# Attention and MLP on one core: the softmax divisor moved to the AV output, scores in three passes

## The chip, the cores and the metric

The kernel runs on one core of one Trainium2 chip. The metric is device time of one execution in microseconds; the median of 3 runs before the change is 752.19 (751.31 to 752.32).

## The reference

Attention over 4 batches, 8 heads, 576 positions and 64 features, with a learned bias of the relative position, and then a two-matrix MLP. Inputs and output are float32.

```
scores = q @ k^T / 8 + bias[h]        # bias[h,i,j] = relu(x*w1+b1) @ w2, x = log1p|i-j| / log1p(max(i,1))
attn   = exp(scores - rowmax)
attn   = attn / (sum(attn) + 1e-9)
x      = attn @ v                     # heads side by side: 2304 rows of 512
out    = (s * relu(x @ w_in)^2 + b) @ w_out     # 512 -> 2048 -> 512
```

## The kernel before

Everything stands in one program whose order on each engine is the order written (a manual schedule); no engine reorders, and all the DMAs named here are issued by SyncE, one after the other.

*Preparation.* The bias is made in 36 stages of 16 rows. A stage (`bias_features`, `bias_step`) makes four feature tiles on VectorE, GpSimd or ScalarE, multiplies them on TensorE (L135, L138), brings the result through ScalarE into a staging tile `stg` (L142) and stores it to `bias_d` in DRAM (L143). Features are written two stages ahead. A table `plan` puts loads and the first two units of attention behind given stages. `load_bias` brings one head's bias back from DRAM: four blocks of 128 rows into `bt`, and the last 64 rows, doubled over the two halves of the partitions, into `be`.

*Attention.* Work goes by pair: one head and two batches, 16 pairs. The two batches lie in the two halves of the partitions of q and k. A pair has five units: units 0 to 3 are 128 query rows of both batches (two score tiles from the 64-row halves of the array), unit 4 the remaining 64 rows of both batches in one tile. `step(n)` does in this order: scores of unit n+2 on TensorE (`scores`, L196); their scaling, bias and row minimum on VectorE (`biased`, L212); the divisor of unit n+1 (`norm`: add, reciprocal, on VectorE, L231 and L232) and its multiplication into the exponents on GpSimd (`norm_scale`, L237); the transposes of unit n on TensorE with their evictions (`probs_t`, L250 to L271: one small transpose evicted by ScalarE, then four evicted by ScalarE, then four evicted by VectorE); the exponents of unit n+2 on ScalarE with their sums (`expo`, L221); a part of the AV product of the pair before (`av`, L283, L286); one or two pieces of weight decoding (`fill`); and loads for later pairs. The transposes share two PSUM buffers, the score tiles two, the AV product has one. At the end of a pair's AV product ScalarE copies it out (L290) and it is stored to DRAM as `xt_d`.

*MLP.* `expand` (L379) and `project` (L403) use three matmuls for each product, of parts that are rounded to a shorter float (F32R) and their remainders. Its weights are decoded and split during attention.

Of the kernel before, what the change touches and what calls it, by code (L numbers as in the profile page):

```python
# [9 lines left out]
F32 = mybir.dt.float32  # L10
# [16 lines left out]
def attention_moe(ctx, tc, q, k, v, w_in, w_out, dist, par, out):  # L27
# [98 lines left out]
    def bias_step(st):  # L126
        f2, f0, f3, f1 = feats.pop(st)
        fs = (f0, f1, f2, f3)
        if st % 3 == 2:
            ps = ps_x.tile([128, 2, 512], F32, tag="x", name="bps")  # L130
        else:
            ps = ps_s.tile([128, 2, 512], F32, tag="s", name="bps")
        pb = ps.rearrange("p a b -> p (a b)")
        for c in range(4):
            nc.tensor.matmul(  # L135
                pb[32 * c:32 * c + 32, 0:512], w2bd, fs[c][0][:, 0:8], start=True, stop=True)
        for c in range(4):
            nc.tensor.matmul(  # L138
                pb[32 * c:32 * c + 32, 512:S], w2bd, fs[c][0][:, 8:9], start=True, stop=True)
        kcol = kc[:, 1:2] if fs[3][1] else kc[:, 0:1]  # L140
        stg = fp.tile([128, S], F32, tag="stg", name="stg", bufs=10)
        nc.scalar.activation(stg, pb[:, 0:S], AF.Identity, scale=nr[:, st:st + 1], bias=kcol)  # L142
        nc.sync.dma_start(out=bias_d[:, 16 * st:16 * st + 16, :].rearrange("h r j -> r h j"), in_=stg)  # L143

# [2 lines left out]


    qs, ks, vals, tts, bts, pts, units, accs = {}, {}, {}, {}, {}, {}, {}, {}

    def load_bias(p, t0, t1):
        h = pairs[p][0]
        if t0 == 0:
            bts[p] = (io.tile([128, 4, S + 64], F32, tag="bt", name="bt"),
                      io.tile([128, S], F32, tag="be", name="be"))
        bt, be = bts[p]
        if t1 <= 4:
            rows = bias_d[h, 128 * t0:128 * t1, :].rearrange("(t p) j -> p t j", p=128)  # L160
            nc.sync.dma_start(out=bt[:, t0:t1, 64:], in_=rows)
            nc.sync.dma_start(out=bt[:, t0:t1, 0:64], in_=rows[:, :, 512:S])
        else:
            nc.sync.dma_start(
                out=be, in_=bias_d[h, 512:S, :].unsqueeze(0).broadcast_to([2, S - 512, S]))

    def load_q(p):
        if p < NP:
            h, b0 = pairs[p]
            qs[p] = io.tile([128, 640], F32, tag="qt", name="qt", bufs=3)  # L170
            nc.sync.dma_start(out=qs[p], in_=q[b0 // 2, h])

    def load_k(p):
        if p < NP:
            h, b0 = pairs[p]
            ks[p] = io.tile([128, S + 64], F32, tag="kt", name="kt", bufs=3)
            nc.sync.dma_start(out=ks[p], in_=k[b0 // 2, h])

    def load_v(p):
        if p < NP:  # L180
# [5 lines left out]
    def scores(n):  # L186
        p, t = divmod(n, 5)
        qt, kt = qs[p], ks[p]
        c = slice(128 * t, 128 * t + 128)
        xs = range(width(n))  # L190
        ps = [ps_s.tile([128, 2, 512], F32, tag="s", name="sps") for _ in xs]
        for hf in range(2):
            for x in xs:
                d = slice(64 * x, 64 * x + 64) if t < 4 else slice(0, 128)
                o = hf * HALF + (64 if x == 0 else 0)
                nc.tensor.matmul(  # L196
                    ps[x][:, hf, 0:HALF], qt[d, c], kt[d, o:o + HALF], start=True, stop=True)
        units[n] = (
            tp.tile([128, 2, S], F32, tag="pr", name="pr"),
            sm.tile([128, 2], F32, tag="mn", name="mn"),  # L200
            sm.tile([128, 2], F32, tag="su", name="su"),
            sm.tile([128, 2], F32, tag="rs", name="rs"),
            ps,
        )

    def biased(n, x):
        p, t = divmod(n, 5)
        _, mn, _, _, ps = units[n]
        bt, be = bts[group[p]]
        bias = bt[:, t, 64 - 64 * x:64 - 64 * x + S] if t < 4 else be  # L210
        tt = tp.tile([128, S], F32, tag="tt", name="tt")
        nc.vector.tensor_tensor_reduce(  # L212
            tt.rearrange("p (a b) -> p a b", a=2), ps[x][:, :, 0:HALF],
            bias.rearrange("p (a b) -> p a b", a=2),
            -1.0 / ROOT, BIG, ALU.add, ALU.min, mn[:, x:x + 1],
        )
        tts[n, x] = tt

    def expo(n, x):
        pr, mn, su, _, _ = units[n]  # L220
        nc.scalar.activation(  # L221
            pr[:, x], tts.pop((n, x)), AF.Exp, bias=mn[:, x:x + 1], scale=-1.0,
            accum_out=su[:, x:x + 1])

    def width(n):
        return 2 if n % 5 < 4 else 1

    def norm(n):
        _, _, su, rs, _ = units[n]
        c = slice(0, width(n))  # L230
        nc.vector.tensor_scalar(su[:, c], su[:, c], 1e-9, None, op0=ALU.add)  # L231
        nc.vector.reciprocal(rs[:, c], su[:, c])  # L232

    def norm_scale(n, x):
        pr, _, _, rs, _ = units[n]
        r = rs[:, x:x + 1]
        nc.gpsimd.tensor_scalar(pr[:, x], pr[:, x], r, 1.0, op0=ALU.mult, op1=ALU.mult)  # L237

    def probs_t(n, part):
        p, t = divmod(n, 5)  # L240
# [7 lines left out]
        if t < 4 and part < 2:  # L248
            for kb in range(4):
                nc.tensor.transpose(  # L250
                    ps[:, 128 * kb:128 * kb + 128],
                    pr[:, part, 64 * part + 128 * kb:64 * part + 128 * kb + 128], ident)
            o, i = pt[:, :, part, c], ps.rearrange("p (a b) -> p a b", a=4)
            if part == 0:
                nc.scalar.activation(o, i, AF.Copy)
            else:
                nc.vector.tensor_copy(o, i)  # L257
        elif t < 4:
            nc.tensor.transpose(ps[:, 0:128], pr.rearrange("p x j -> p (x j)")[:, 512:640], ident)  # L259
# [12 lines left out]

    def av(p, kb, hf):
# [12 lines left out]
            nc.tensor.matmul(ps[:, hf, 0:HALF], vt[:, 8:10].rearrange("p i d -> p (i d)"), ptr[:, c],  # L286
                             start=False, stop=True)
        if kb == 4 and hf == 1:
            xs = tp.tile([128, S], F32, tag="xs", name="xs", bufs=1)
            nc.scalar.activation(xs.rearrange("p (a b) -> p a b", a=2), ps[:, :, 0:HALF], AF.Copy)  # L290
            nc.sync.dma_start(out=xt_d[b0 // 2][:, h * D:(h + 1) * D, :], in_=xs)


# [127 lines left out]
    for p, (h, _) in enumerate(pairs):  # L421
        group.append(next(i for i, e in enumerate(pairs) if e[0] == h))
        if group[p] == p and p > 0:
            loads_at[p - 2, 2] = ((p, 0, 4), (p, 4, 5))

    def step(n):
        p, u = divmod(n, 5)
# [19 lines left out]
        if p >= 1:  # L447
# [2 lines left out]
            fill()  # L450
            if u % 2 == 0:
                fill()
        if n < LAST:
# [21 lines left out]
    def fill():  # L475
# [23 lines left out]
    }  # L499
    for st in range(STEPS):  # L500
        if st + 2 < STEPS:
# [47 lines left out]
    op = ctx.enter_context(tc.tile_pool(name="op", bufs=2, reuse_waits="tile"))  # L549
    wa = ctx.enter_context(tc.tile_pool(name="wa", bufs=1, reuse_waits="tile"))  # L550
    for kind in range(2):
        alloc_w(w_hi, kind, 1, wa)
# [11 lines left out]
        next(work)  # L564
    pctx.close()
    ps_ctx.close()
    w2 = ctx.enter_context(tc.tile_pool(name="w2", bufs=1, reuse_waits="tile"))
    for kind in range(2):
        alloc_w(w_hi, kind, 2, w2)
# [97 lines left out]
```

## Time and profile before

| | |
|---|---|
| median of 3 runs | 752.19 us |
| profiled execution | 752.64 us |
| its span | 750.8 us |
| mean granted clock of TensorE | 0.993 of full |
| preparation | 0 to about 54 us |
| attention | to about 348 us |
| MLP | to the end |
| TensorE, weight loads, VectorE, ScalarE, GpSimd busy | 97%, 70%, 58%, 50%, 29% of the span |

The page gives shares of the whole span. TensorE's ends are modelled, so that a start of the next group of instructions is the better measure of a duration than a busy time. "Idle before" is followed by what released the engine. Lines L*n* are lines of the kernel before.

### The profile page before, as it was taken

Reading aid. Unit: us, or ns where it says so; the run is one execution under the profiler, and the core shown is the slowest. Engines: PE = TensorE matmul, PEld = TensorE weight load, DVE = VectorE, ACT = ScalarE, POOL = GpSimd, SP = SyncE. Lnnn points to the kernel's source line nnn. Section 1 sums busy time; section 2 is a strip of 40 time slices with the busy share of each in tenths; the row PEclk is TensorE's granted clock in tenths of the full one; section 3 lists DMA queues with packets and bytes.
Section 4 is the critical chain, followed back from the end, with each engine's and each line's share of the span. In section 5 each row is a group of like instructions: output and inputs, shape, how many; then the busy total and the mean of one; then the engine's idle time right before and its main releaser. Section 6 shows DMA issues by size and latency. Waiting matters only on the chain.

```text
span 750.8 us, 11513 instructions
## 1 busy us (share of the span) xinstructions
PE 730.1 (97%) x4226; PEld 526.9 (70%) x4226; DVE 431.9 (58%) x890; ACT 375.1 (50%) x772; POOL 218.7 (29%) x274
## 2 busy tenths in 40 slices
PE   8985999999999999999999999999999999999998
PEld 4443665666666666656888888888888888888896
DVE  7973778888878787883379732233322333223332
ACT  7983677677777777775444422223222232222332
POOL 7962455465445444452664200000000000000000
PEclk9997999999999999999999999999999999999999
DMA  5996344446354654224012130000300002000100
GB/s 170 289 334 198 129 148 160 168 140 196 112 203 130 213 179 180 69 66 142 13 57 81 33 101 12 1 1 0 113 1 0 1 0 85 1 0 1 57 1 28
DMA packets 36056, 71.56 MB, mean 95 GB/s; under 512 B 7712, under 2 KB 10912, under 8 KB 36000
## 3 DMA queue, kind: packets, MB, share of 16 engines
q1 hardware_dynamic: 35856, 70.51, 28.3%
q8 instruction: 33, 0.54, 0.3%
q10 hardware_dynamic: 144, 0.33, 0.1%
q14 instruction: 23, 0.19, 0.1%
HBM read 50.77 MB, written 20.05 MB: 94 GB/s over the span
## 4 chain that ended last, share of the span: by engine, by line
PE 82%; DVE 7%; DMA 3%; ACT 3%; POOL 2%; issue 1%; POOLq 0%; ACTq 0%; DVEq 0%
PE hps L379 27%; PE o L403 27%; PE sps L196 9%; PE xps L283 8%; PE tps L250 6%; PE bps L135 3%; DVE tt L212 3%; POOL pr L237 2%; DMA bias<-stg 2%; PE tps L259 1%; DMA be<-bias 1%; ACT pr L221 1%; ACT stg L142 1%; DVE full L329 1%; PE xps L286 1%
## 5 line engine op out<-in xcount | busy, mean ns | idle before, releaser
L403 PE MATMUL o<-who,gt 128*128 128x512 f32 x576 | 192.4, 393 | 0.0
L379 PE MATMUL hps<-x,whi 128*128 128x512 f32 (+1 forms) x640 | 183.7, 371 | 0.0
L384 DVE SCALAR_TENSOR_TENSOR r<-r,sb 128x512 f32<-128x512 f32 (+1 forms) x80 | 56.8, 709 | 193.5 <-ACT r L383 193.5
L383 ACT ACTIVATE r<-hps 128x512 f32<-128x512 f32 (+1 forms) x80 | 44.4, 555 | 221.9 <-PE hps L379 221.9
L237 POOL TENSOR_SCALAR pr<-pr,rs 128x576 f32<-128x576 f32 x144 | 109.4, 771 | 145.6 <-DVE rs L232 113.5
L379 PEld LDWEIGHTS hps<-x,whi 128*128 128x128 f32 x640 | 116.9, 188 | 23.9 <-issue 0.4
L403 PEld LDWEIGHTS o<-who,gt 128*128 128x128 f32 x576 | 108.2, 188 | 24.1
L221 ACT ACTIVATE pr<-tt,mn 128x576 f32<-128x576 f32 x144 | 110.7, 771 | 20.2 <-DVE su L231 15.8
L379 PE MATMUL hps<-x,wli 128*128 128x512 f32 (+1 forms) x320 | 118.7, 371 | 0.0
L196 PE MATMUL sps<-kt,qt 64*128 64x288 f32 (+1 forms) x576 | 108.4, 433 | 9.7 <-DVE mn L212 9.4
L403 PE MATMUL o<-wlo,gt 128*128 128x512 f32 x288 | 113.2, 393 | 0.0
L212 DVE CUSTOM_DVE_ANT_0 tt<-sps,bt 128x576 f32<-128x576 f32 x128 | 95.6, 747 | 25.9 <-PE sps L196 25.8
L196 PEld LDWEIGHTS sps<-kt,qt 64*128 64x128 f32 (+1 forms) x576 | 62.6, 188 | 51.2 <-DVE mn L212 17.5
L389 DVE SCALAR_TENSOR_TENSOR gt<-r,sb,gt 128x512 fp32r<-128x512 f32 (+1 forms) x80 | 56.3, 703 | 54.2 <-ACT gt L388 54.2
L388 ACT ACTIVATE gt<-r,sb 128x512 fp32r<-128x512 f32 (+1 forms) x80 | 54.4, 681 | 52.5 <-DVE r L384 52.5
L250 PE MATMUL tps<-ident,pr 128*128 128x128 f32 x512 | 77.2, 282 | 1.5 <-ACT ptr L260 1.5
L283 PE MATMUL xps<-pt,vt 128*64 128x288 f32 x512 | 75.8, 418 | 0.0
L379 PEld LDWEIGHTS hps<-x,wli 128*128 128x128 f32 x320 | 60.1, 188 | 10.9
L250 PEld LDWEIGHTS tps<-ident,pr 128*128 128x128 f32 x512 | 57.7, 142 | 13.4 <-ACT ptr L260 12.5
L403 PEld LDWEIGHTS o<-wlo,gt 128*128 128x128 f32 x288 | 54.1, 188 | 11.7
L283 PEld LDWEIGHTS xps<-pt,vt 128*64 128x64 f32 x512 | 31.2, 136 | 23.9 <-issue 10.8
L257 DVE COPY pt<-tps 128x512 f32<-128x512 f32 x64 | 44.0, 687 | 5.8 <-PE tps L250 5.0
(63 smaller groups left out, 700.1 us busy)
## 6 DMA issues: line engine op xcount, KB each, us to landing
bias<-stg SPq DMA_DIRECT2D x36, 288.0 KB
raw<-in_moe_w_in_dram SPq DMA_DIRECT2D x16, 512.0 KB
raw<-in_moe_w_out_dram SPq DMA_DIRECT2D x16, 512.0 KB
bt<-bias SPq DMA_DIRECT2D x7, 1152.0 KB
qt<-in_q_dram SPq DMA_DIRECT2D x16, 320.0 KB
kt<-in_k_dram SPq DMA_DIRECT2D x16, 320.0 KB
vt<-in_v_dram SPq DMA_DIRECT2D x16, 320.0 KB
xt<-xs SPq DMA_DIRECT2D x16, 288.0 KB
```

The costliest lines, as they stand in the source:

```text
L196: nc.tensor.matmul(ps[x][:, hf, 0:HALF], qt[d, c], kt[d, o:o + HALF], start=True, stop=True)
L212: nc.vector.tensor_tensor_reduce(tt.rearrange("p (a b) -> p a b", a=2), ps[x][:, :, 0:HALF], bias.rearrange("p (a b) -> p a b", a=2), -1.0 ...
L221: nc.scalar.activation(pr[:, x], tts.pop((n, x)), AF.Exp, bias=mn[:, x:x + 1], scale=-1.0, accum_out=su[:, x:x + 1])
L237: nc.gpsimd.tensor_scalar(pr[:, x], pr[:, x], r, 1.0, op0=ALU.mult, op1=ALU.mult)
L250: nc.tensor.transpose(ps[:, 128 * kb:128 * kb + 128], pr[:, part, 64 * part + 128 * kb:64 * part + 128 * kb + 128], ident)
L283: nc.tensor.matmul(ps[64 * x:64 * x + 64, hf, 0:HALF], vt[:, 4 * x + kb, :], pt[:, kb, x, c], start=(kb == 0), stop=False)
L379: nc.tensor.matmul(ps[:, 0:n], w[0, g][:, a, fc], xs_t[c, a][:, j, 0:n], start=(i == 0), stop=(i == 3 * KB - 1))
L383: nc.scalar.activation(r, ps[:, 0:n], AF.Relu)
L384: nc.vector.scalar_tensor_tensor(r, r, sb[:, 0:1], r, op0=ALU.mult, op1=ALU.mult)
L388: nc.scalar.activation(hi, r, AF.Identity, bias=sb[:, 1:2])
L389: nc.vector.scalar_tensor_tensor(lo, r, sb[:, 1:2], hi.bitcast(F32), op0=ALU.add, op1=ALU.subtract)
L403: nc.tensor.matmul(os_t[c][i], gt[:, a, tok], w[1, g][:, fo], start=(f == 0 and j == 0), stop=(f == NF - 1 and j == 2))
```

## The change

The scores are made from q and k split into a rounded part and a remainder: three passes in place of one float32 matmul; the splits are made on GpSimd, two for each pair. The probabilities stay undivided through transposes and AV product. The nine columns of sums of a pair are inverted once (`norm`, in the step of unit 3), transposed on TensorE (`norm_t`), copied out by VectorE, stored to DRAM (`norm_store`), loaded back spread over 64 partitions for each batch (`norm_load`, in the step of unit 4) and multiplied into the AV product as it leaves PSUM, on VectorE, in place of ScalarE's copy. The bias tile's last 64 rows are loaded once per head, as two transfers of 64 rows; for the first head, stages 24 to 35 are sent directly from the staging tile (`first_head`). Loads of the preparation are moved, q and k have two buffers in place of three, and the output pool is opened later.

```diff
@@ bias_step
+        if st >= 24:
+            first_head(st, stg)
         nc.sync.dma_start(out=bias_d[:, 16 * st:16 * st + 16, :].rearrange("h r j -> r h j"), in_=stg)
+    def first_head(st, stg):
+        bt, be = bts[0], bes[0]
+        t, r0 = divmod(16 * st, 128)
+        rows = stg[0:128:H, :]
+        if t < 4:
+            nc.sync.dma_start(out=bt[r0:r0 + 16, t, 64:], in_=rows)
+            nc.sync.dma_start(out=bt[r0:r0 + 16, t, 0:64], in_=rows[:, 512:S])
+        else:
+            for x in range(2):
+                nc.sync.dma_start(out=be[64 * x + r0:64 * x + r0 + 16, :], in_=rows)
@@ loads
-            nc.sync.dma_start(
-                out=be, in_=bias_d[h, 512:S, :].unsqueeze(0).broadcast_to([2, S - 512, S]))
+    def load_be(p):
+        if p == 0:
+            bes[0] = io.tile([128, S], F32, tag="be", name="be", bufs=1)
+        elif p < NP and pairs[p][0] == pairs[p - 1][0]:
+            bes[p] = bes[p - 1]
+        elif p < NP:
+            bes[p] = io.tile([128, S], F32, tag="be", name="be", bufs=1)
+            for x in range(2):
+                nc.sync.dma_start(out=bes[p][64 * x:64 * x + 64, :], in_=bias_d[pairs[p][0], 512:S, :])
-            qs[p] = io.tile([128, 640], F32, tag="qt", name="qt", bufs=3)
+            qs[p] = io.tile([128, 640], F32, tag="qt", name="qt")
-            ks[p] = io.tile([128, S + 64], F32, tag="kt", name="kt", bufs=3)
+            ks[p] = io.tile([128, S + 64], F32, tag="kt", name="kt")
+    def split_qk(p, which):
+        if p < NP:
+            full = (qs, ks)[which][p]
+            t = io.tile([128, 2, 640], F32R, tag=f"r{which}", name="qr" if which == 0 else "kr")
+            nc.gpsimd.tensor_scalar(t[:, 0], full, 1.0, 1.0, op0=ALU.mult, op1=ALU.mult)
+            nc.gpsimd.tensor_tensor(t[:, 1], full, t[:, 0].bitcast(F32), op=ALU.subtract)
+            (qs, ks)[which][p] = t
@@ scores
+        mms = []
         for hf in range(2):
             for x in xs:
                 d = slice(64 * x, 64 * x + 64) if t < 4 else slice(0, 128)
                 o = hf * HALF + (64 if x == 0 else 0)
-                nc.tensor.matmul(
-                    ps[x][:, hf, 0:HALF], qt[d, c], kt[d, o:o + HALF], start=True, stop=True)
+                for i, (a, b) in enumerate(((0, 0), (0, 1), (1, 0))):
+                    mms.append((i, hf, x, ps[x][:, hf, 0:HALF], qt[d, a, c], kt[d, b, o:o + HALF]))
+        for i, _, _, o, a, b in sorted(mms, key=lambda e: e[1::-1]):
+            nc.tensor.matmul(o, a, b, start=(i == 0), stop=(i == 2))
@@ divisor
-    def norm(n):
-        _, _, su, rs, _ = units[n]
-        c = slice(0, width(n))
-        nc.vector.tensor_scalar(su[:, c], su[:, c], 1e-9, None, op0=ALU.add)
-        nc.vector.reciprocal(rs[:, c], su[:, c])
-    def norm_scale(n, x):
-        pr, _, _, rs, _ = units[n]
-        r = rs[:, x:x + 1]
-        nc.gpsimd.tensor_scalar(pr[:, x], pr[:, x], r, 1.0, op0=ALU.mult, op1=ALU.mult)
+    def norm(p):
+        su = sums.pop(p)
+        nc.vector.tensor_scalar(su, su, 1e-9, None, op0=ALU.add)
+        nc.vector.reciprocal(su, su)
+        rows[p] = su
+    def norm_t(p, ps):
+        nc.tensor.transpose(ps[0:9, 128:256], rows.pop(p), ident)
+        rt = sm.tile([9, 128], F32, tag="rt", name="rt", bufs=2)
+        nc.vector.tensor_copy(rt, ps[0:9, 128:256])
+        rts[p] = rt
+    def norm_store(p):
+        rt = rts.pop(p)
+        for x in range(2):
+            nc.sync.dma_start(
+                out=rs_d[p][x, 0:512].rearrange("(t j) -> t j", j=128), in_=rt[4 * x:4 * x + 4, :])
+            nc.sync.dma_start(out=rs_d[p][x:x + 1, 512:S], in_=rt[8:9, 64 * x:64 * x + 64])
+    def norm_load(p):
+        rbs[p] = tp.tile([128, S], F32, tag="rb", name="rb", bufs=2)
+        for x in range(2):
+            nc.sync.dma_start(out=rbs[p][64 * x:64 * x + 64, :], in_=rs_d[p][x:x + 1, :].broadcast_to([D, S]))
@@ probs_t
             nc.scalar.activation(ptr[:, c], ps[:, 0:128], AF.Copy)
+            if t == 3:
+                norm_t(p, ps)
@@ av
-            xs = tp.tile([128, S], F32, tag="xs", name="xs", bufs=1)
-            nc.scalar.activation(xs.rearrange("p (a b) -> p a b", a=2), ps[:, :, 0:HALF], AF.Copy)
+            xs = rbs.pop(p)
+            xv = xs.rearrange("p (a b) -> p a b", a=2)
+            nc.vector.tensor_tensor(xv, ps[:, :, 0:HALF], xv, op=ALU.mult)
@@ step
             biased(m, 0)
-        if ok(n + 1, 0):
-            norm(n + 1)
-            norm_scale(n + 1, 0)
-            if ok(n + 1, 1):
-                norm_scale(n + 1, 1)
+        if cur and u == 3:
+            norm(p)
         if ok(m, 1):
             biased(m, 1)
...
             if u == 3:
+                load_be(p + 1)
                 load_q(p + 3)
                 load_k(p + 3)
+                norm_store(p)
+            if u == 4:
+                norm_load(p)
+            if u < 2:
+                split_qk(p + 1, u)
@@ plan
-        20: ((load_v, 0), (load_q, 2)),
-        23: ((load_k, 2), (load_v, 1)),
+        20: ((load_v, 0), (load_be, 0)),
+        28: ((split_qk, 0, 0),),
+        30: ((split_qk, 0, 1),),
         26: ((load_bias, 0, 2, 3),),
-        29: ((load_w, *early[0]),),
-        32: ((load_w, *early[1]),),
-        33: ((load_bias, 0, 3, 4), (scores, 0), (biased, 0, 0), (expo, 0, 0), (biased, 0, 1)),
-        35: ((load_bias, 0, 4, 5), (expo, 0, 1), (scores, 1), (biased, 1, 0),
-             (norm, 0), (norm_scale, 0, 0), (expo, 1, 0), (biased, 1, 1),
-             (norm_scale, 0, 1), (expo, 1, 1)),
+        33: ((scores, 0), (biased, 0, 0), (expo, 0, 0), (biased, 0, 1)),
+        35: ((expo, 0, 1), (scores, 1), (biased, 1, 0),
+             (expo, 1, 0), (biased, 1, 1), (expo, 1, 1), (load_w, *early[0]), (load_w, *early[1]),
+             (load_q, 2), (load_k, 2), (load_v, 1)),
```

## Rows read from the trace of the kernel before

**Rows 1.** The page: busy time, share of span, instructions, by engine.
```profile
PE 730.1 (97%) x4226; PEld 526.9 (70%) x4226; DVE 431.9 (58%) x890; ACT 375.1 (50%) x772; POOL 218.7 (29%) x274
```
**Rows 2.** Busy time by stretch: us, engines, granted clock, DMA share, GB/s.
```profile
84.00:334.00 250.00, 247.55 (x1608) 152.55 (x1609) 209.27 (x547) 178.34 (x435) 121.25 (x159) 1.00 0.44 150
...
348.00:751.00 403.00, 399.14 (x1824) 328.07 (x1823) 152.80 (x207) 126.48 (x216) 40.57 (x32) 1.00 0.09 28
```
**Rows 3.** TensorE in time order: start, us, instructions, idle before.
```profile
72.62 2.29 PE L196 MATMUL sps<-kt,qt 64*128 64x288 f32 x6 [7.88 <-DVE mn L212]
```
**Rows 4.** VectorE in order of time, the same place.
```profile
71.80 0.76 DVE L212 CUSTOM_DVE_ANT_0 tt<-sps,be 128x576 f32<-128x576 f32 x1 [9.45 <-DMA be<-bias]
```
**Rows 5.** SyncE's DMA issues in order of time, before that wait.
```profile
56.54 0.33 SPq L161 DMA_DIRECT2D bt<-bias  x1
...
57.44 1.17 SPq L143 DMA_DIRECT2D bias<-stg  x2
61.92 0.62 SPq L164 DMA_DIRECT2D be<-bias  x1
```
**Rows 6.** Busy time by stretch, behind the idle time.
```profile
72.60:77.50 4.90, 4.88 (x17) 3.46 (x19) 2.91 (x10) 2.44 (x7) 2.21 (x3) 0.50 0.87 262
```
**Rows 7.** TensorE in time order: first and last of 72 scores.
```profile
83.90 1.24 PE L196 MATMUL sps<-kt,qt 64*128 64x288 f32 x8
...
333.88 0.99 PE L196 MATMUL sps<-kt,qt 128*128 128x288 f32 x3
```
**Rows 8.** TensorE in time order, units 2 to 4 of a pair.
```profile
211.82 1.24 PE L196 MATMUL sps<-kt,qt 128*128 128x288 f32 x4
...
215.24 1.24 PE L196 MATMUL sps<-kt,qt 64*128 64x288 f32 x8
216.41 0.33 PE L259 MATMUL tps<-ident,pr 128*128 128x128 f32 x1
...
217.69 1.19 PE L283 MATMUL xps<-pt,vt 128*64 128x288 f32 x8
218.81 1.24 PE L196 MATMUL sps<-kt,qt 64*128 64x288 f32 x8
...
221.62 1.46 PE L196 MATMUL sps<-kt,qt 64*128 64x288 f32 x8
```
**Rows 9.** Waits between 80 and 330 us: total, times, longest.
```profile
PEld tps L259 <- POOL pr L237: 16.5, 39, 0.8
```
**Rows 10.** GpSimd: its order in the preparation, and its subtractions of 512 columns.
```profile
27.57 20.88 POOL L118 TENSOR_SCALAR f<-ls,thr 128x576 f32<-128x576 f32 x29
...
L344 POOL TENSOR_TENSOR wli<-full,whi 128x512 fp32r<-128x512 f32 x16 | 23.4, 1469 | 17.7 <-ACT whi L343 15.0 <-DVE whi L341 2.6
```
**Rows 11.** GpSimd and VectorE in order of time, late in attention.
```profile
328.46 0.62 POOL L324 TENSOR_SCALAR full<-full 128x512 f32<-128x512 f32 x1 [1.11 <-ACT full L322]
328.49 0.61 DVE L231 TENSOR_SCALAR su<-su 128x2 f32<-128x2 f32 x1
```
**Rows 12.** TensorE in time order, bias stage 33 and first scores.
```profile
46.77 1.44 PE L135 MATMUL bps<-f,pt__94 128*32 128x512 f32 x8
...
48.25 0.75 PE L196 MATMUL sps<-kt,qt 64*128 64x288 f32 x2
```
**Rows 13.** The chain of work: MLP groups of 512 and 256 columns.
```profile
453.40 2.73 PE hps L379 x12
...
696.23 1.42 PE hps L379 x12
```
**Rows 14.** VectorE in order of time, unit 3 of the same pair.
```profile
216.51 0.76 DVE L212 CUSTOM_DVE_ANT_0 tt<-sps,bt 128x576 f32<-128x576 f32 x1 [0.89 <-PE sps L196]
...
217.19 0.15 DVE L231 TENSOR_SCALAR su<-su 128x1 f32<-128x1 f32 x1
217.38 0.16 DVE L232 RECIPROCAL rs<-su 128x1 f32<-128x1 f32 x1
...
218.12 0.69 DVE L257 COPY pt<-tps 128x512 f32<-128x512 f32 x1
```

More of the change, by code (lines that the diff above doesn't have):

```diff
@@ L60, in attention_moe @@
     bias_d = dram.tile([H, S, S], F32, name="bias")
+    rs_d = [dram.tile([2, S], F32, name=f"rs{p}") for p in range(NP)]
     xt_d = [dram.tile([2, DM, S], F32, name=f"xt{b}") for b in range(NB // 2)]
@@ L142, in bias_step @@
         nc.scalar.activation(stg, pb[:, 0:S], AF.Identity, scale=nr[:, st:st + 1], bias=kcol)
+        if st >= 24:
+            first_head(st, stg)
         nc.sync.dma_start(out=bias_d[:, 16 * st:16 * st + 16, :].rearrange("h r j -> r h j"), in_=stg)
+    def first_head(st, stg):
[8 more added lines that the diff above has]
+                nc.sync.dma_start(out=be[64 * x + r0:64 * x + r0 + 16, :], in_=rows)
     qs, ks, vals, tts, bts, pts, units, accs = {}, {}, {}, {}, {}, {}, {}, {}
+    sums, rows, rts, rbs, bes = {}, {}, {}, {}, {}
     def load_bias(p, t0, t1):
@@ L155, in load_bias @@
         if t0 == 0:
[L156 to L163, printed above, removed]
-            nc.sync.dma_start(
-                out=be, in_=bias_d[h, 512:S, :].unsqueeze(0).broadcast_to([2, S - 512, S]))
+            bts[p] = io.tile([128, 4, S + 64], F32, tag="bt", name="bt")
+        bt = bts[p]
+        rows = bias_d[h, 128 * t0:128 * t1, :].rearrange("(t p) j -> p t j", p=128)
+        nc.sync.dma_start(out=bt[:, t0:t1, 64:], in_=rows)
+        nc.sync.dma_start(out=bt[:, t0:t1, 0:64], in_=rows[:, :, 512:S])
+    def load_be(p):
[7 more added lines that the diff above has]
+                nc.sync.dma_start(out=bes[p][64 * x:64 * x + 64, :], in_=bias_d[pairs[p][0], 512:S, :])
     def load_q(p):
@@ L200, in scores @@
             sm.tile([128, 2], F32, tag="mn", name="mn"),
-            sm.tile([128, 2], F32, tag="su", name="su"),
-            sm.tile([128, 2], F32, tag="rs", name="rs"),
-            ps,
-        )
+            ps,
+        )
+        if t == 0:
+            sums[p] = sm.tile([128, 9], F32, tag="su", name="su")
     def biased(n, x):
         p, t = divmod(n, 5)
-        _, mn, _, _, ps = units[n]
-        bt, be = bts[group[p]]
-        bias = bt[:, t, 64 - 64 * x:64 - 64 * x + S] if t < 4 else be
+        _, mn, ps = units[n]
+        bias = bts[group[p]][:, t, 64 - 64 * x:64 - 64 * x + S] if t < 4 else bes[p]
         tt = tp.tile([128, S], F32, tag="tt", name="tt")
@@ L219, in expo @@
     def expo(n, x):
-        pr, mn, su, _, _ = units[n]
+        p, t = divmod(n, 5)
+        pr, mn, _ = units[n]
+        col = 4 * x + t if t < 4 else 8
         nc.scalar.activation(
             pr[:, x], tts.pop((n, x)), AF.Exp, bias=mn[:, x:x + 1], scale=-1.0,
-            accum_out=su[:, x:x + 1])
+            accum_out=sums[p][:, col:col + 1])
     def width(n):
         return 2 if n % 5 < 4 else 1
-    def norm(n):
-        _, _, su, rs, _ = units[n]
-        c = slice(0, width(n))
-        nc.vector.tensor_scalar(su[:, c], su[:, c], 1e-9, None, op0=ALU.add)
-        nc.vector.reciprocal(rs[:, c], su[:, c])
-    def norm_scale(n, x):
-        pr, _, _, rs, _ = units[n]
-        r = rs[:, x:x + 1]
-        nc.gpsimd.tensor_scalar(pr[:, x], pr[:, x], r, 1.0, op0=ALU.mult, op1=ALU.mult)
+    def norm(p):
[18 more added lines that the diff above has]
+            nc.sync.dma_start(out=rbs[p][64 * x:64 * x + 64, :], in_=rs_d[p][x:x + 1, :].broadcast_to([D, S]))
     def probs_t(n, part):
@@ L423, in attention_moe @@
         if group[p] == p and p > 0:
-            loads_at[p - 2, 2] = ((p, 0, 4), (p, 4, 5))
+            loads_at[p - 2, 2] = ((p, 0, 4),)
     def step(n):
@@ L452, in step @@
                 fill()
-        if n < LAST:
+        if 0 <= n < LAST:
             if u == 3:
+                load_be(p + 1)
                 load_q(p + 3)
                 load_k(p + 3)
+                norm_store(p)
[3 more added lines that the diff above has]
+                split_qk(p + 1, u)
             if u == 4:
@@ L548, in attention_moe @@
     xp = ctx.enter_context(tc.tile_pool(name="xp", bufs=1, reuse_waits="tile"))
-    op = ctx.enter_context(tc.tile_pool(name="op", bufs=2, reuse_waits="tile"))
     wa = ctx.enter_context(tc.tile_pool(name="wa", bufs=1, reuse_waits="tile"))
@@ L566, in attention_moe @@
     ps_ctx.close()
+    op = ctx.enter_context(tc.tile_pool(name="op", bufs=2, reuse_waits="tile"))
     w2 = ctx.enter_context(tc.tile_pool(name="w2", bufs=1, reuse_waits="tile"))
```

## Prediction

> **What bounds the kernel now.** I read the page first, then busy time by stage, then TensorE's order of work at three places, then the engine that ends each wait there. TensorE is busy 730.1 us of a span of 750.8 [rows 1]. By stage [rows 2]: from 84 to 334 us (attention) TensorE has 247.55 of 250 us, VectorE 209.27, ScalarE 178.34, GpSimd 121.25; from 348 on (the MLP) TensorE has 399.14 of 403 us and nothing the change touches. So an edit counts where it changes TensorE's work or makes TensorE wait in attention, or where it moves the preparation ahead of it. The profiled execution took 752.64 us, span plus 1.8 around it; the median of the runs is 752.19, so the sum below, made against 752.64, carries over less 0.45.
>
> Between preparation and attention TensorE is idle 7.88 us [rows 3]: scores wait for a PSUM tile that VectorE frees, and VectorE is idle 9.45 us until the DMA of `be` has landed [rows 4]. Its chain is SyncE's: the load of the bias tile's fourth block is issued at 56.54, two bias stores come behind it, and `be` is issued at 61.92 [rows 5]. After the idle time the granted clock is 0.50, the 1.2 GHz level, for 72.6 to 77.5 us [rows 6].
>
> In attention, a step runs scores, transposes, then the AV product. 71 steps take 333.88 - 83.90 = 249.98 us [rows 7], 17.60 us for a pair of five. One pair without waits, from [rows 8]: unit 2 takes 215.24 - 211.82 = 3.42, unit 3 takes 3.57, unit 4 takes 2.81; with units 0 and 1 built as unit 3, 16.94. So 0.66 us a pair is waiting. Its largest piece is unit 0: its scores group lasts 1.46 where others last 1.24, because its next transpose waits for GpSimd's scaling, a wait found 39 times [rows 9].
>
> **The change, part by part.** *The gap.* The first head's last rows now go from the SBUF staging tile straight into `bt` and `be`, so `be` no longer waits for the store to DRAM and a load behind it. Removed: 9.45 us. The slow-clock stretch goes with the idle time: 4.88 us of TensorE work at half the level, 2.44 at the full one; as ScalarE and VectorE also pace those steps I take 2.0. What is late next: 24 new DMAs on SyncE (two for each of 12 stages), while eight leave the stretch or move behind the last bias store (three bias loads; two weight blocks, q, k and v of later pairs, first needed some five steps later, so costed at nothing). Issues took 0.33 to 0.62 us [rows 5], so 16 more cost 5 to 10 us of SyncE over twelve stages. Today its last bias stores are issued from 57.44 to 58.61, behind a load that the change takes away; the last rows now go out ahead of them and are wanted at 71.80 - 9.45 = 62.35, or four microseconds later with the splits below. Price 0, and 9.45 if SyncE falls that far behind. Sum -11.45.
>
> *Splits in the preparation.* Four new GpSimd instructions, q and k, each a copy and a subtraction of 640 columns. From 512 columns: 1.469 x 1.25 = 1.84 for the subtraction [rows 10] and 0.62 x 1.25 = 0.78 for the copy [rows 11], together 2 x 2.62 = 5.2 us. GpSimd has no idle there: 29 features back to back in 20.88 us, 0.72 each, the last ending at 48.45 [rows 10]. Stage 33 needs the feature four before the last, which ended at 48.45 - 4 x 0.72 = 45.6, and its matmul started at 46.77 [rows 12]. So 1.2 us are covered: +4.0 (0 if later features have more slack, 5.2 if none).
>
> *Scores.* A 64-row group now has eight instructions that run in four side-by-side pairs, 1.17 us from 215.24 to 216.41 [rows 8]. Afterwards there are twelve instructions of the round-float kind, six pairs. Such an instruction costs 2.73 / 12 = 0.2275 us for 512 columns and 1.42 / 12 = 0.118 for 256 [rows 13], so 0.132 for 288. The old slots at two passes of 288 columns (0.245) leave 1.17 - 4 x 0.245 = 0.19 for start and end; the new group is 6 x 0.132 + 0.19 = 0.98: -0.18. The 128-row group of unit 2 has six instead of four instructions, and I give it the same. About 75 groups lie where TensorE sets the pace: -13.5. No row shows 64-row pairs of this kind: between -0.25 a group and, if pairs don't run side by side, 12 x 0.132 + 0.19 - 1.17 = +0.60.
>
> *The divisor's transpose.* This is the new wait. In unit 3 the sums of the pair are inverted on VectorE behind the first biased score tile of the same step, and TensorE, in order, transposes them right after the small transpose. Clock from the start of that step's scores. VectorE began the biased tile 1.27 us in (216.51) and the reciprocal 0.87 later, taking 0.16 [rows 14]; with scores 0.18 shorter the rows are ready at 1.09 + 1.03 = 2.12, while TensorE got there at 1.15. The new transpose ends near 2.33. The next four transposes use the other PSUM buffer, but the four after them need the buffer that holds the transposed divisor, and VectorE copies that out only behind the second biased tile: its next instruction started 1.61 after the first began [rows 14], so at 2.70, plus 0.25 for 128 columns (512 take 0.69). Queued behind it are those four transposes (0.58 with their start), the AV product and the next scores. AV starts at 3.0 + 0.58 = 3.58 instead of 217.69 - 215.24 - 0.18 = 2.27: 1.3 us. Fifteen pairs have scores beside it: +19.5. Least: 0.85 (first wait alone), most 1.9 (VectorE behind by one more 0.6 us instruction).
>
> *Scaling leaves GpSimd, its wait goes.* Nothing stands between exponent and transpose now. Of 0.66 us waiting a pair I take 0.36 as gone (unit 0's 0.22 and ScalarE's eviction ahead of the small copy); the rest is VectorE's backlog from weight decoding. 14.2 pairs: -5.1 (0 to -9.4).
>
> *At nothing.* The AV eviction moves from ScalarE to VectorE, about 0.75 us by VectorE's 0.69 for a 512-column eviction [rows 14]; the same unit loses two small instructions each step, and the accumulator is wanted again more than two microseconds later. Without that cover, 0.75 x 15 = +11 at most. Per pair SyncE gets four small stores (waiting for VectorE) and two broadcast loads (waiting for the stores); behind them stand loads wanted a step or more later, and the rows are multiplied a whole pair, 17 us, after; even the slowest landing here, `be`'s, took 71.80 - 61.92 = 9.9 us [rows 4, 5]. GpSimd's splits per pair, 5.2 us, replace nine scalings. Two q and k buffers instead of three, `be` loaded once per head in two halves, and the output pool's later place cost nothing as long as each stays a step ahead; a miss would cost its own few microseconds once per pair.
>
> Sum: -11.45 + 4.0 - 13.5 + 19.5 - 5.1 = -6.55, 746.1 against the profiled execution, 745.6 against the median. I predict 746.
>
> **Rivals.** *1. The lock on the other side: slower.* VectorE's first small divisor instruction took 0.61 us where a GpSimd instruction of 0.62 ran beside it [rows 11], against 0.15 where none did [rows 14]: the two engines shut each other out. GpSimd's new subtraction lasts 1.84. Where it stands in unit 3 as the divisor is inverted, TensorE waits for both: up to 1.7 x 15 = +25, 771; at one microsecond, 761. It decides from 6.55 / 15 = 0.44 us a pair. Against it: the splits are written behind units 0 and 1 and GpSimd has little queued ahead of them. 0.13. The Trainium skill ("SBUF — State Buffer", "Who interferes with whom") says that GpSimd and a VectorE instruction in a two-port mode take a shared port pair in turn and the later one blocks for the other's whole instruction; the 0.61 us agree.
>
> *2. Pairs one after the other: slower.* +0.60 instead of -0.18 on 60 groups of 64 rows: +47, 793. Against it: the eight instructions of today overlap in pairs. 0.05.
>
> *3. The gap stays: the change doesn't do what it says there.* SyncE falls behind and `be` lands as late against its need as before: -6.55 + 9.45 = +2.9, 755; half of it is 750. For it: SyncE has 16 more issues in a busy stretch. 0.10.
>
> *4. Better covered: faster.* Splits hidden in the preparation (-4.0) and all waits gone (-4.3): 738; with the shorter wait of 0.85 as well, 731. For it: ScalarE and VectorE both lose work. 0.20.
>
> **How the numbers follow.** The forecast has 0.52; its own range is 741 to 752. A measurement tells about 0.2%, 1.5 us, from no change. Faster: 0.48 of the forecast, 0.20 of rival 4, 0.02 of 3: 0.70. Same: 0.03 of the forecast, 0.05 of 3: 0.08. Slower: rivals 1 and 2, the rest of 3 and of the forecast: 0.22. The range goes from 735 (half of rival 4 outside) to 759 (rival 3 inside, most of rivals 1 and 2 out).
>
> **What would show it.** Right: no VectorE wait for `be`, granted clock 1.00 from 60 to 80 us; the first score group four microseconds later than 48.25; scores groups near 0.98; in each unit 3 TensorE stands about 1.3 us in two waits for VectorE, the second for the divisor's copy; pairs of about 17.5 us; the MLP as long as before. Wrong: unit 3 without that wait, score groups above 1.17, or a new wait for `rb` or `be`.

## The result, and the profile after

The changed kernel takes 759.02 us (758.64 to 760.7, 4 runs) against 752.25: a ratio of 1.0097, 95% interval 1.008 to 1.0115. It is one per cent slower, clear of the scatter, where 746 and faster were forecast. Medians are over executions in the fast state; one of the ten of e9_split_two_steps_earlier (2383.24 us) is not among them. The profiled execution took 759.01 us with a span of 757.0, 6.2 more than before.

TensorE in time order, first and last of the same 72 score groups of the changed kernel (start, us, instructions, idle before), to set beside [rows 7]:

```profile
77.50 1.06 PE L228 MATMUL sps<-kr,qr 64*128 64x288 f32 x12
...
340.15 1.07 PE L228 MATMUL sps<-kr,qr 128*128 128x288 f32 x6
```

Up to the first of them the kernel gained 83.90 - 77.50 = 6.4 us. Between the two it lost 12.7 us: 340.15 - 77.50 = 262.65 us against 249.98. From the last of them to the end of the span nothing changed (416.85 against 416.92). The sum is the +6.2.

The starts of the score groups between give each step's length. Mean of 14 or 15 steps, before and after: unit 0 3.94 and 3.42, unit 1 3.68 and 3.59, unit 2 3.56 and 3.30, unit 4 2.83 and 2.67; unit 3 3.57 and 5.52. All but unit 3 became shorter, 14.5 us together; unit 3 alone grew by 27.2. Its median is 4.94, and four of the 14 took 7.29, 8.10, 7.27 and 5.43.

An ordinary unit 3 of the changed kernel, TensorE in time order, for [rows 8]:

```profile
236.18 1.06 PE L228 MATMUL sps<-kr,qr 64*128 64x288 f32 x12
237.17 0.33 PE L307 MATMUL tps<-ident,pr 128*128 128x128 f32 x1
238.62 0.27 PE L270 MATMUL tps<-ident,su 128*9 128x128 f32 x1 [1.12 <-DVE su L266]
238.72 1.32 PE L298 MATMUL tps<-ident,pr 128*128 128x128 f32 x8
239.97 1.19 PE L333 MATMUL xps<-pt,vt 128*64 128x288 f32 x8
241.10 1.07 PE L228 MATMUL sps<-kr,qr 64*128 64x288 f32 x12
```

VectorE in the same stretch, for [rows 14]:

```profile
237.37 0.76 DVE L242 CUSTOM_DVE_ANT_0 tt<-sps,bt 128x576 f32<-128x576 f32 x1 [0.45 <-PE sps L228]
...
238.25 0.21 DVE L266 RECIPROCAL su<-su 128x9 f32<-128x9 f32 x1
238.39 0.75 DVE L242 CUSTOM_DVE_ANT_0 tt<-sps,bt 128x576 f32<-128x576 f32 x1
...
239.06 0.27 DVE L272 COPY rt<-tps 9x128 f32<-9x128 f32 x1
```

The score group takes 237.17 - 236.18 = 0.99 us where it took 1.17. Then TensorE stands for 1.12 us, to 238.62, because VectorE has inverted the sums only at 238.25 + 0.21 = 238.46, and again, inside the group of eight transposes (1.32 us in place of 1.19), until VectorE has copied the divisor out (239.06 + 0.27 = 239.33).

One of the long unit 3s, TensorE in time order:

```profile
102.04 0.40 PE L228 MATMUL sps<-kr,qr 64*128 64x288 f32 x2
103.23 0.93 PE L228 MATMUL sps<-kr,qr 64*128 64x288 f32 x10 [0.79 <-POOL kr L204]
104.09 0.33 PE L307 MATMUL tps<-ident,pr 128*128 128x128 f32 x1
105.55 0.37 PE L270 MATMUL tps<-ident,su 128*9 128x128 f32 x1 [1.13 <-DVE su L266]
105.72 1.91 PE L298 MATMUL tps<-ident,pr 128*128 128x128 f32 x8
107.56 1.84 PE L333 MATMUL xps<-pt,vt 128*64 128x288 f32 x8
```

Busy time by stretch of the changed kernel (us, then PE, PEld, DVE, ACT, POOL, granted clock, DMA share, GB/s), for [rows 2, 6]:

```profile
105.50:108.90 3.40, 3.35 (x15) 2.47 (x17) 1.97 (x5) 2.09 (x5) 0.00 (x0) 0.50 0.17 60
143.10:149.80 6.70, 5.71 (x28) 3.76 (x30) 3.19 (x9) 2.39 (x6) 0.00 (x0) 0.50 0.25 77
184.10:187.40 3.30, 3.30 (x15) 1.56 (x14) 0.69 (x2) 2.67 (x6) 0.45 (x1) 0.50 0.16 57
84.00:334.00 250.00, 229.93 (x1779) 154.82 (x1779) 195.15 (x440) 158.26 (x397) 86.00 (x83) 0.97 0.51 168
```

Here a second wait stands ahead of the divisor's: the scores wait 0.79 us for GpSimd's split of k. Behind the two waits the granted clock is 0.50, the 1.2 GHz level, and the same eight transposes take 1.91 us and the AV group 1.84 instead of 1.19. Three such stretches are 13.4 us together. The second, from 143.1 us, begins behind k's wait but ahead of the divisor's. TensorE in time order:

```profile
142.15 0.92 PE L228 MATMUL sps<-kr,qr 64*128 64x288 f32 x10 [1.27 <-POOL kr L204]
143.00 0.47 PE L307 MATMUL tps<-ident,pr 128*128 128x128 f32 x1
144.46 0.37 PE L270 MATMUL tps<-ident,su 128*9 128x128 f32 x1 [0.99 <-DVE su L266]
```

k's split is late because of what stands ahead of it on GpSimd, a subtraction of weights that waits 5.93 us for VectorE. GpSimd in time order, before the unit 3 at 102 us:

```profile
99.58 1.28 POOL L395 TENSOR_TENSOR wli<-full,whi 128x512 fp32r<-128x512 f32 x1 [5.93 <-DVE whi L392]
100.83 0.73 POOL L203 TENSOR_SCALAR kr<-kt 128x640 fp32r<-128x640 f32 x1
101.64 1.54 POOL L204 TENSOR_TENSOR kr<-kt,kr 128x640 fp32r<-128x640 f32 x1
```

At the start of attention, first VectorE, then SyncE's issues (start, us, times issued at the end) of the changed kernel in time order, for [rows 4, 5]:

```profile
67.06 0.76 DVE L242 CUSTOM_DVE_ANT_0 tt<-sps,be 128x576 f32<-128x576 f32 x1 [1.93 <-DMA be<-stg]
```
```profile
53.32 0.59 SPq L146 DMA_DIRECT2D bias<-stg  x1
54.02 0.54 SPq L153 DMA_DIRECT2D bt<-stg  x1
54.59 0.59 SPq L154 DMA_DIRECT2D bt<-stg  x1
...
64.05 1.18 SPq L157 DMA_DIRECT2D be<-stg  x2
```

The 9.45 us have become 1.93, and the slow-clock stretch ahead of attention is gone in this execution (granted clock 1.00 from 48 to 84 us). It does not stay away: e1 and e2 below, with the same preparation, show 6.8 us at 0.50 from 52.5 and from 69.6 us. What remains is SyncE's: 24 issues of mostly 0.54 to 0.59 us, one after the other with the bias stores, put the last ones at 64.05, and the rows land after that.

### The profile page after: what moved, and what is told of

The parts are those of the page before. It is cut to its first block, busy times and chain, and to the rows that moved or that the text cites. A ratio compares the mean times of both kernels' runs of the same rounds, so it can differ in the third digit from the quotient of the medians.

```text
span 757.0 us, 12033 instructions
## 1 busy us (share of the span) xinstructions
PE 722.6 (95%) x4530; PEld 538.3 (71%) x4530; DVE 428.3 (57%) x794; ACT 362.5 (48%) x756; POOL 185.4 (24%) x194
## 4 chain that ended last, share of the span: by engine, by line
PE 81%; POOL 6%; DVE 5%; issue 4%; DMA 2%; SPq 1%; ACT 1%; POOLq 0%; DVEq 0%
PE hps L430 26%; PE o L454 26%; PE sps L228 8%; PE xps L333 7%; PE tps L298 7%; POOL f L119 4%; DVE tt L242 3%; PE xps L336 2%; PE tps L307 1%; PE tps L313 1%; DMA raw<-in_moe_w_in_dram 1%; PE tps L318 0%; SPq L154 0%; DMA pt__110<-in_par_dram 0%; POOL kr L204 0%
## 5 line engine op out<-in xcount | busy, mean ns | idle before, releaser
L253 ACT ACTIVATE pr<-tt,mn 128x576 f32<-128x576 f32 x144 | 110.2, 767 | 13.9 <-DVE mn L242 13.4
L242 DVE CUSTOM_DVE_ANT_0 tt<-sps,bt 128x576 f32<-128x576 f32 x128 | 92.3, 749 | 39.6 <-PE sps L228 34.8
L228 PEld LDWEIGHTS sps<-kr,qr 64*128 64x128 f32 (+1 forms) x864 | 69.5, 187 | 42.1 <-DVE mn L242 16.9
L228 PE MATMUL sps<-kr,qr 64*128 64x288 f32 (+1 forms) x864 | 90.9, 313 | 6.5 <-POOL kr L204 2.9
L298 PE MATMUL tps<-ident,pr 128*128 128x128 f32 x512 | 79.6, 285 | 0.9 <-ACT ptr L308 0.3
L333 PE MATMUL xps<-pt,vt 128*64 128x288 f32 x512 | 78.4, 430 | 0.0
L298 PEld LDWEIGHTS tps<-ident,pr 128*128 128x128 f32 x512 | 58.5, 144 | 13.4 <-ACT ptr L308 9.0
L303 ACT ACTIVATE pt<-tps 128x512 f32<-128x512 f32 x64 | 38.3, 598 | 32.0 <-PE tps L298 30.3
L375 POOL TENSOR_SCALAR full<-full 128x512 f32<-128x512 f32 x32 | 21.0, 657 | 127.0 <-ACT full L373 120.6
```

What stands on the lines that cost most here:

```text
L228: nc.tensor.matmul(o, a, b, start=(i == 0), stop=(i == 2))
L242: nc.vector.tensor_tensor_reduce(tt.rearrange("p (a b) -> p a b", a=2), ps[x][:, :, 0:HALF], bias.rearrange("p (a b) -> p a b", a=2), -1.0 ...
L253: nc.scalar.activation(pr[:, x], tts.pop((n, x)), AF.Exp, bias=mn[:, x:x + 1], scale=-1.0, accum_out=sums[p][:, col:col + 1])
L298: nc.tensor.transpose(ps[:, 128 * kb:128 * kb + 128], pr[:, part, 64 * part + 128 * kb:64 * part + 128 * kb + 128], ident)
L333: nc.tensor.matmul(ps[64 * x:64 * x + 64, hf, 0:HALF], vt[:, 4 * x + kb, :], pt[:, kb, x, c], start=(kb == 0), stop=False)
```

## The experiments

The theory after the result: the divisor's transpose, in the place where it stands, costs TensorE about 1.5 us a pair, and where k's split is late as well the two waits together bring the clock down. Rivals: GpSimd's splits and SyncE's issues are the loss; or the lighter scores bring the clock down.

**e1_invert_early.** `norm` moved ahead of the step's scores and first biased tile.

```diff
+        if cur and u == 3:
+            norm(p)
         if ok(m, 0):
             scores(m)
             biased(m, 0)
-        if cur and u == 3:
-            norm(p)
```

> The divisor is inverted on VectorE ahead of the step's first biased tile instead of behind it; its copy out of PSUM stays behind the second biased tile. If the wait in unit 3 is what cost the time: the first wait (1.13 us, 15 times) goes, the second stays at about 0.8, unit 3 falls from 4.9 to about 4.3 us, 15 x 0.6 = 9 us less than the changed kernel's 759, 750; if the granted clock then stays at 1.00 another 8 less, 742. If the loss lies in GpSimd's splits and SyncE's queue: 757 to 760, unit 3 still near 4.9.

755.88 us (752.28 to 758.83), 1.0043 of before (1.0023 to 1.0063). The gain is a third of what was expected: unit 3 has a median of 4.80, only 0.14 less, and the granted clock still falls in two unit 3s with a late split, and once ahead of attention. TensorE in time order:

```profile
236.05 0.33 PE L307 MATMUL tps<-ident,pr 128*128 128x128 f32 x1
236.74 0.28 PE L270 MATMUL tps<-ident,su 128*9 128x128 f32 x1 [0.37 <-ACT ptr L308]
236.86 0.60 PE L298 MATMUL tps<-ident,pr 128*128 128x128 f32 x4
238.15 0.66 PE L298 MATMUL tps<-ident,pr 128*128 128x128 f32 x4 [0.69 <-ACT pt L303]
```

Here the wait for the inversion is gone (three of 14 pairs still have one, of 0.5 us), and two others stand in its place: for ScalarE's eviction of the small transpose that shares the divisor's PSUM tile (L308), and, before the last four transposes, for a PSUM buffer that ScalarE frees (L303). The divisor's transpose waits for a read of other columns of its tile, which the prediction had not seen; in the changed kernel that wait lies under the longer one.

**e2_copy_on_scalar.** The other half alone.

```diff
-        nc.vector.tensor_copy(rt, ps[0:9, 128:256])
+        nc.scalar.activation(rt, ps[0:9, 128:256], AF.Copy)
```

> The copy of the transposed divisor goes to ScalarE, which is behind nothing there; the inversion stays behind the first biased tile. If unit 3's wait is the cause: the first wait stays (1.1 us), the second nearly goes; unit 3 about 4.5 to 4.6, 15 x 0.35 = 5 us less than 759, 754, with the drops of the granted clock left or gone (746 to 754). If VectorE's copy was not in TensorE's way: 759 and unit 3 as before at 4.9.

756.31 us (751.29 to 761.02), 1.004 (1.0013 to 1.0068): within what was expected, unit 3 at 4.81 where 4.5 to 4.6 stood, so the second wait alone is worth 0.13 us. Its clock falls four times in the profiled execution. How often it falls differs between executions of one kernel: the ten here go from 751.29 us at a mean granted clock of 0.999 to 761.02 at 0.985. So unit 3's median tells more of these edits than the time.

**e3_both.** Both edits together.

> Both: divisor inverted ahead of the first biased tile and copied out by ScalarE. If unit 3's two waits and the clock drops that follow them are the whole loss of attention: unit 3 about 3.55 us (3.40 and one more transpose), clock 1.00 throughout, 759 - 15 x 1.35 - 8 = 731 (729 to 736). If the clock drops come from the lighter scores and not from that wait: 739. If the loss lies elsewhere: above 750.

742.79 us (742.03 to 744.16), 0.9868 (0.9843 to 0.9893): a gain of 16 us, where 28 were expected. Unit 3 has a median of 4.03, 0.91 less than in the changed kernel, where the edits alone took off 0.14 and 0.13: the waits hide each other. One drop of the clock is left (3.4 us, at a unit 3 of 7.02 us in which k's split is late too). What is left of unit 3 above 3.40 (3.57 less the 0.17 that the scores gained) is again the shared tile:

```profile
225.49 0.33 PE L307 MATMUL tps<-ident,pr 128*128 128x128 f32 x1
226.18 0.28 PE L270 MATMUL tps<-ident,su 128*9 128x128 f32 x1 [0.37 <-ACT ptr L308]
226.30 1.18 PE L298 MATMUL tps<-ident,pr 128*128 128x128 f32 x8
```

**e4_pair0_float32.** The first pair's scores in float32; its four splits leave the preparation.

```diff
-        28: ((split_qk, 0, 0),),
-        30: ((split_qk, 0, 1),),
...
+                if p == 0:
+                    nc.tensor.matmul(ps[x][:, hf, 0:HALF], qt[d, c], kt[d, o:o + HALF], start=True, stop=True)
+                    continue
```

> The first pair's scores are made in float32 as before, so that its four splits leave GpSimd in the preparation; all else as in the changed kernel. If those splits delay the preparation: the first score group is back near 48.3 from 51.9 us and the time 3.5 us less, 755.5, plus 0.8 for five slower score groups. If the preparation is held by VectorE or ScalarE, or SyncE's issues for the bias rows then end it: 758 to 760.

758.58 us (754.26 to 759.75), 1.006 (1.0037 to 1.0083). The second answer: the first scores start at 48.48 instead of 51.93, so the splits do delay the preparation by 3.5 us, but VectorE then waits 4.37 us for `be`, and the slow level is back (0.50 from 66.5 for 6.8 us).

```profile
66.31 0.76 DVE L245 CUSTOM_DVE_ANT_0 tt<-sps,be 128x576 f32<-128x576 f32 x1 [4.37 <-DMA be<-stg]
```

**e5_scores_float32.** All scores in float32, no splits, three q and k buffers; the diff is that of e4_pair0_float32 for every pair and without `split_qk` in the steps.

> All scores in float32 as before, no splits, three q and k buffers; the rest as in the changed kernel. The three-pass scores gain 0.17 us a group, 80 groups, 13.6 us; if their splits on GpSimd give most of it back (k's split late for unit 3 four times, about 4 us, and the three drops of the granted clock, about 8): 757 to 763 against 759, no drop of the clock in attention. If the splits cost nothing there and the clock drops come from the divisor's wait alone: 770 to 773, with the drops still there.

761.03 us (759.77 to 761.45), 1.0109 (1.0091 to 1.0127): the first answer. No drop of the clock in attention, with unit 3 at 5.07 in every pair: the divisor's wait alone doesn't bring it down. Every score group is 0.17 us slower, some 13 us in all, and yet the kernel is only 2.0 us slower: the splits and the drops of the clock had cost nearly what the lighter scores gained. The run does not tell the parts of its edit (splits in the preparation, late splits, buffers) from one another.

**e6_first_rows_alone.** The kernel before with `first_head` alone, without the two loads that it replaces; every other load stays.

> The kernel before with one part of the change: stages 24 to 35 send the first head's rows directly, the two loads of them from DRAM are gone; every other load stays. If the gap ahead of attention is a real cost: VectorE's wait for be falls from 9.45 us to 3 to 5 (SyncE has 24 more issues of 0.6 us and the rows land late), 744 to 748 against 752.9, more if the granted clock then stays at 1.00. If another wait takes its place: 751 to 753.

751.14 us (750.15 to 752.78), 0.9979 (0.9969 to 0.9988): the second answer, a gain of 1.6 us where 5 to 9 stood in the first. VectorE in time order:

```profile
61.88 0.76 DVE L225 CUSTOM_DVE_ANT_0 tt<-sps,bt 128x576 f32<-128x576 f32 x1 [2.46 <-DMA bt<-stg]
...
70.55 0.76 DVE L225 CUSTOM_DVE_ANT_0 tt<-sps,be 128x576 f32<-128x576 f32 x1 [6.10 <-DMA be<-stg]
```

One wait of 9.45 us has become two, 8.56 together. SyncE's queue, not the way through DRAM, now sets when the rows arrive: its issues run one behind the other, the last of `be` from 67.37 us.

**e9_split_two_steps_earlier.** q and k of a pair are split behind units 3 and 4 two pairs ahead, not behind units 0 and 1 of the pair before.

```diff
-            if u < 2:
-                split_qk(p + 1, u)
+            if n < 2:
+                split_qk(1, u)
+            if u >= 3:
+                split_qk(p + 2, u - 3)
```

> q and k of a pair are split two steps earlier; the divisor as in the changed kernel. If the granted clock falls where the wait for k's split and the divisor's wait come together: no drop in attention, unit 3 about 4.9 us in every pair, 759 - 8 - 4 = 747 (745 to 750). If the divisor's wait alone makes the clock fall: the drops stay, 754 to 756.

751.27 us (749.99 to 754.06), 0.9988 (0.9972 to 1.0004): 7.8 us off, not the 12 expected. The 12 counted the late splits twice: in the changed kernel the four long unit 3s lie 8.3 us above the median in all, the lower clock included. In attention there is no drop, with unit 3 at 4.93 and the divisor's wait, up to 1.38 us, in each pair. Busy time by stretch:

```profile
84.00:334.00 250.00, 231.46 (x1844) 156.31 (x1843) 198.93 (x455) 164.42 (x412) 84.97 (x83) 1.00 0.52 172
```

So the divisor's wait alone does not bring the clock down, nor do the lighter scores, which are all in this kernel; k's late split is a condition. (The clock was low for 6.8 us from 68 us, ahead of attention, in this profiled execution.)

**e10_transpose_one_step_later.** The transpose moves to unit 4, ahead of the small transpose in that one's PSUM tile; store and load one step later.

```diff
-            if t == 3:
-                norm_t(p, ps)
...
+            norm_t(p, ps)
             nc.tensor.transpose(ps[0:64, 0:128], pr[:, 0, 512:S], ident)
```

> The divisor's transpose moves to the step of unit 4, first in the PSUM tile of the small transpose, its store and load one step later; splits as in the changed kernel. If the three waits around that transpose (VectorE's inversion, ScalarE's eviction of the tile it shares, the tile's release) are the loss: unit 3 near 3.4 but where k's split is late (four times 4.3 to 5), unit 4 near 2.75, no drop of the clock, 759 - 15 x 1.4 - 8 = 730 (728 to 735). If the drops come from the wait for k's split: 734 to 738.

765.33 us (763.38 to 766.35), 1.0161 (1.014 to 1.0182): a miss. TensorE in time order, one pair and the last:

```profile
236.10 0.28 PE L270 MATMUL tps<-ident,su 128*9 128x128 f32 x1
237.89 0.30 PE L317 MATMUL tps<-ident,pr 128*64 128x128 f32 x1 [1.52 <-DVE rt L272]
...
342.56 0.28 PE L270 MATMUL tps<-ident,su 128*9 128x128 f32 x1
348.80 0.42 PE L317 MATMUL tps<-ident,pr 128*64 128x128 f32 x1 [5.96 <-DVE rt L272]
```

Unit 3 fell to 3.39, as expected, but the next transpose into the shared tile now waits for VectorE's copy of the divisor, which stands behind two biased tiles: unit 4 has 4.42 instead of 2.63. In the last pair that copy stands behind the splits of the MLP's input, 5.96 us, and the clock falls to 0.50 for 6.8 us. The wait has moved with the shared tile.

**e12_own_tile_after_av.** A PSUM tile of its own, behind the AV product of unit 3; all else as in the changed kernel.

```diff
-    def norm_t(p, ps):
+    def norm_t(p):
+        ps = ps_t.tile([128, 512], F32, tag="t", name="nps")
         nc.tensor.transpose(ps[0:9, 128:256], rows.pop(p), ident)
...
             av(p - 1, u, 1)
+        if cur and u == 3:
+            norm_t(p)
+        if p >= 1:
             fill()
```

> The divisor's transpose gets a PSUM tile of its own and stands behind the AV product of the step of unit 3; inversion, store, load and splits as in the changed kernel. If its place in a shared PSUM tile, between transposes that TensorE runs in order, is the loss: unit 3 near 3.5 (3.40 and one transpose), but for the pairs in which k's split is late, and no drop of the granted clock since the two waits no longer meet: 759 - 15 x 1.4 - 8 = 730 (728 to 736). If the divisor cannot be hidden anywhere in the step: another step takes the 1.4 us over, above 750.

735.25 us (734.34 to 737.82), 0.9773 (0.9749 to 0.9798): as expected. TensorE in time order:

```profile
219.98 0.33 PE L308 MATMUL tps<-ident,pr 128*128 128x128 f32 x1
220.14 1.19 PE L299 MATMUL tps<-ident,pr 128*128 128x128 f32 x8
221.26 1.19 PE L332 MATMUL xps<-pt,vt 128*64 128x288 f32 x8
222.38 0.28 PE L271 MATMUL nps<-ident,su 128*9 128x128 f32 x1
222.59 1.05 PE L228 MATMUL sps<-kr,qr 64*128 64x288 f32 x12
```

No wait is left in these rows, unit 3 has a median of 3.60 and unit 4 is as short as in the changed kernel (2.62). Tile and place changed together here; what each is worth alone was not run.

The granted clock is 1.00 from 84 to 334 us though k's split is late in the same pairs (unit 3 up to 5.14). That the drops need the divisor's wait as well is not shown, for three reasons: the stretch from 143.1 us in the changed kernel began ahead of that wait; nearly the same two waits were followed by a drop in the changed kernel (0.61 and 1.18 us) and by none in e4 (0.63 and 1.19); and two of the four executions here, without a profile, have a mean clock of 0.997 and 0.995.

**e13_own_tile_early_split, e14_best_guess, e15_be_alone_direct.** e13 is e12 and e9 together. e15 is e13 with only the four `be` stages sent directly (`st >= 32`) and `bt`'s fourth block loaded from DRAM at stage 33. e14 is e15 with the first pair's scores in float32.

> The same, and q and k split two steps earlier. If the late split of k is a loss of its own: 3 to 4 us below the run without it, 726 to 730, with unit 3 near 3.5 in every pair. If it only mattered through the clock: as that run.

> The same, with the first pair's scores in float32 (no splits in the preparation) and only the four stages of be sent directly, bt's fourth block from DRAM as before. If GpSimd's splits and SyncE's 24 issues hold the end of the preparation: VectorE's wait for be gone, first scores near 48.3, 720 to 724. If one of the two takes the other's place: 725 to 730.

> The kernel of e13_own_tile_early_split with only the four stages of be sent directly: 16 issues less on SyncE, the splits stay in the preparation. If SyncE's queue makes be late (1.9 us of waiting): 2 us below e13. If the load of bt from DRAM makes SyncE wait for the stores again: the same or 1 to 3 above.

731.87 us (731.79 to 732.18), 0.9724 (0.9709 to 0.9738); 726.9 us (726.75 to 727.0), 0.9656 (0.9639 to 0.9673); and 730.98 us (730.32 to 732.86), 0.9715 (0.9695 to 0.9736). k's late split is a loss of its own: 3.4 us at the median (735.25 to 731.87), 2.5 between executions with a mean clock of 1.00. Unit 3 is 3.6 in every pair of e13, as expected, though its time lies above 726 to 730, as e12's lay above 730. Fewer direct rows gain 0.9 us at the most, within the scatter. With the splits out of the preparation too, 4.1 us more, where taking out the splits alone had gained 0.4 (e4, with the divisor in its old place): there the two hold each other. In e14 VectorE no longer waits for `be`, and the first scores start at 48.35, yet its time is that of the second answer, 725 to 730:

```profile
62.02 0.76 DVE L245 CUSTOM_DVE_ANT_0 tt<-sps,be 128x576 f32<-128x576 f32 x1 [0.21 <-PE tps L311]
```

e14 beats both kernels: 3.4% under the kernel before, 4.2% under the changed one (726.9 / 759.02).

## Why the prediction was wrong

The step that failed is one that stood *at nothing*: the splits of q and k in attention, which were to cost nothing as long as each stays a step ahead. They don't. In four pairs k's split came late, and in three of these the granted clock fell to 0.50; that puts unit 3's mean above its median, 5.52 against 4.94, 8.1 us over 14 pairs. With the splits two steps earlier (e9) 7.8 us are gone. The prediction compared GpSimd's work in total and not what stands ahead of a split: three of the late ones come behind a subtraction of weights that waits 5.9 to 10.4 us for VectorE, the fourth behind a piece of weight decoding that waits 11.9 us for ScalarE. And no wait of TensorE was priced with the clock, though [rows 6] showed what follows idle time.

A second term was too small: *the divisor's transpose*, priced at +19.5. The place and the two waits were as forecast; the size was 4.94 - 3.57 + 0.17 (what the scores gained) = 1.54 us a pair where 1.3 stood, 3.4 us over 14 pairs. Counted from the start of the step's scores, the inverted sums were ready at 2.28 us (forecast 2.12), their copy began at 2.88 (2.70) and the AV product at 3.79 (3.58): VectorE began 0.10 us later than forecast, its inversion took 0.05 more, and TensorE started 0.16 after it ended.

The other terms. *The gap*: forecast -11.45, and with the splits -7.45; measured -6.4. Rival 3 was partly right: SyncE made `be` late by 1.93 us, by 4.37 with the splits gone (e4), and in e6 took nearly all of the gain. The 16 more issues cost 0.54 to 0.59 us each, the upper part of the range. *Splits in the preparation*: +4.0 forecast, first scores 48.25 to 51.93, +3.7. *Scores*: -0.18 a group forecast, 0.99 against 1.17. Rival 2 is out: twelve rounded 64-row instructions take 0.99 us, where it gave them 1.77 one after another. *Scaling's wait*: -5.1 forecast; units 0, 1, 2 and 4 became 14.5 us shorter, of which 57 groups x 0.17 = 9.7 are scores, so -4.8 by difference. *Rival 1* didn't happen: the longest of 14 waits for the inversion was 1.2 us. *Rival 4* did not happen in the changed kernel; times like its 738 and 731 came only with the divisor's transpose in a tile and place of its own (735.25 and 731.87).

So of the miss of 13 us (759 against 746), 11.5 come from unit 3 (8.1 + 3.4) and 1.1 from the start of attention. The divisor's way through DRAM, which carries the change's name, shows no wait: no engine waits for `rb` in the changed kernel.

The Trainium skill ("TensorE: Matmul & The Clock Gate", "HAM oscillation — how this bites in real kernels") says that waits between bursts of matmuls can bring the slow clock back each time. The changed kernel's trace agrees where the lower clock came back in three unit 3s, as behind the waits of 0.79 and 1.13 us; in e9 a wait of up to 1.38 us in each unit 3 did not bring it back.

## What to carry to other kernels

Work moved to an engine with time to spare can still come late: look at what stands ahead of it there and what that waits for, not at the engine's total. Before a small operation is put between two groups of an engine that takes its work in order, list everything that its tile makes it wait for, and what waits for the tile afterwards; three such waits hid one another here, and taking one away gained 0.14 us of 1.54. With a buffer of its own and a place behind long work it cost 0.20 here (unit 3 at 3.60 against 3.40 without it). And allow for the clock when TensorE's waits stand close together: here it fell behind some of them, not in every execution.

## What was not expected of the hardware

Two waits of TensorE of 0.79 and 1.13 us, their ends 2.3 us apart, were followed by 3.4 us at a granted clock of 0.50; the divisor's wait alone, in every pair of e9, was not. Nearly equal waits differed: 0.61 and 1.18 us in the changed kernel were followed by a drop, 0.63 and 1.19 in e4 were not. An issue of a transfer of 16 rows took SyncE 0.54 to 0.59 us, as long as the 0.59 of the 288 KB store of 128 rows. In e6, where the first head's last rows no longer go through DRAM, two waits of VectorE of 8.56 us together stood in place of one of 9.45, and the time fell by 1.6 us only.
